# Eight sets of sums for w_out: where in the kernel they are made and written

## The chip, the cores and the metric

The kernel runs on one core of a Trainium2 chip. The core has five engines with queues of their own: TensorE (PE) for matmuls, VectorE (DVE), ScalarE (ACT), GpSimd (POOL), and SyncE (SP), which issues all of this kernel's DMAs in one order. Sixteen DMA engines carry the transfers. Each engine runs its own instructions in order, and engines wait for each other by semaphores. The metric is the device time of one execution in microseconds (us), as a median of several runs.

## The reference

Attention within chunks of 64 tokens, followed by a feed-forward layer with ELU, all in float32:

```python
# q, k, v: [8 batches, 8 heads, 576 tokens, 64], chunks of 64 tokens
scores = scale * np.matmul(q_c, k_c.transpose(0, 1, 2, 4, 3))
scores = scores - np.max(scores, axis=-1, keepdims=True)
attn = np.exp(scores)
attn = attn / (np.sum(attn, axis=-1, keepdims=True) + 1e-09)
x = np.matmul(attn, v_c)             # then reshaped to [4608 tokens, 512]
...
h = x @ w_in                          # w_in: [512, 2048]
g = np.where(h > 0.0, h, np.exp(np.minimum(h, 0.0)) - 1.0)
return g @ w_out                      # w_out: [2048, 512]
```

## The kernel before

**Numbers.** Each float32 operand of a large matmul is split into a high and a low part of a narrower float type, and a product is three matmuls (`three`, L431): high times high, high times low, low times high. The split is always the same pair of instructions: ACT copies the high part, and DVE or POOL subtracts it to get the low part.

**Blocks.** The 4608 tokens are nine blocks of 512. Three go through the plain way. The other six are three *superblocks* of two blocks each. There the two products with w_in are done by a scheme with 7 instead of 8 block products (Strassen's, in Winograd's form). For a pair g of 128-wide slices of the hidden layer (f = 2g and 2g + 1; eight pairs), `PRODUCTS` names the operands: parts and sums of w_in from `a_dram` in DRAM, and parts and sums of x. In the third superblock the product with w_out is done in the same way, and that needs *sums of w_out*.

**The sums of w_out.** `Sums` (L564) makes one set for a pair j of 128-row slices of w_out, j = 0 to 7. The steps are: `whole` twice (high plus low gives the float32 slice, 128x512), `sum` four times (differences of quarter matrices, 128x256), `high` (ACT, 128x1024), `low` (128x1024), and `write`: two DMAs of 512 KB each to `w_dram`, the high parts and the low parts. `whole` reads the low parts of w_out from `weights[0][3]`, a ring that holds eight of the sixteen slices at a time and is refilled from `lo_dram` by `load_lo` (L666) after each odd f is used. A set needs a place of 128 x 2048 floats. The other operands of the last superblock are unsummed parts, which `write_raw` ("W0" to "W5", 512 KB each) and `write_raw_low` ("L0" to "L7", 384 KB each) send to `w_dram`.

**The first two superblocks** (`for sb in range(2)`, L1363) have an order written out by hand. Each has two stages:

- *Pairs* (L1366): `FIRST_PAIR`, `SECOND_PAIR` and six times `PAIR` are strings of items. `p1` to `p7` are the seven products into two PSUM banks. Each product also issues the load of the same operand for the next pair (`load_a`, L650, 256 KB). `c` and `d` take products out of PSUM, `1` to `4` apply ELU and split the result, and `Q` is one quarter of a product with w_out. Between them runs the attention for the tokens of the next superblock, one tile of 128 tokens per pair: `l` loads q and k into one of two staging places `kept_st[0]` and `kept_st[1]` (L227, eight or sixteen small DMAs), `q` and `k` turn them, `s` multiplies them, `m E z h` make the weights and turn them with four swap DMAs (L399) at the end, `v` multiplies by v (`times_v`, L256), and `V` loads the next v (L206). In a pair the order on PE is p1, p2, p6, p5, p7, p4, p3, then s and v.
- *The second half* (`KEPT`, sixteen rows f = 0 to 15): the second block's g, kept in `g_kept`, is split (`split_kept`, L811: ACT high, then the low part on the engine that its last lines choose) and multiplied with w_out, four `Q` a row, two rows after the split. Rows also hold the attention and the preparation of the next superblock's x operands (`x...` items, L688 to L697).

Before the change, four sets (j = 0 to 3) are made in the *second* superblock's pairs: `SUMS_AT` names the items after which `do("w")` takes one more step of `combine_w_out`. Wholes and differences are on POOL, `high` on ACT, `low` on DVE, and both halves are written at once. The sets lie in rows 8 to 15 of `g_kept`. The raw parts are written in the second half of that superblock, as `RAW` says.

**The last superblock** is ordered by a planner (`Plan`, L824). Jobs have an engine or a choice of two, a cost, and the keys that they read and write; a job is due a little before the first PE job that needs it, and each engine takes the ready job that is due first. `add_sums` (L1835) adds the sets j = 4 to 7 there, staged in the place of `g_more`. The operands come through a ring of four slots of 512 KB (`load_entry`), whose first four loads are the items R0 to R3 of the second superblock's second half.

Of the kernel before, what the change touches and what calls it, by code (L numbers as in the profile page):

```python
# [20 lines left out]
def kernel(  # L21
# [542 lines left out]
    class Sums:  # L564
# [8 lines left out]
        def whole(self, i: int, engine=nc.gpsimd):  # L573
            engine.tensor_tensor(  # L574
                out=self.w[:, i], in0=w_out_slices(2 * self.j + i)[0].bitcast(F32),
                in1=self.lows[i].bitcast(F32), op=ALU.add)

        def sum(self, t: int, engine=nc.gpsimd):
            b11, b12, b21, b22 = [self.w[:, i, c * HALF:(c + 1) * HALF]
                                  for i in range(2) for c in range(2)]  # L580
            t1, t2, t3, t4 = [self.s[:, i] for i in range(4)]
            out, a, b = ((t1, b12, b11), (t2, b22, t1), (t3, b22, b12), (t4, b21, t2))[t - 1]
            engine.tensor_tensor(out=out, in0=a, in1=b, op=ALU.subtract)
# [8 lines left out]

        def write(self):
            for lo in range(2):
                nc.sync.dma_start(
                    out=w_dram[:4, self.j // 2, :, self.j % 2, lo, :].rearrange("i p w -> p i w"),
                    in_=self.place[:, lo].rearrange("p (i d) -> p i d", i=4))

    def combine_w_out():
        for j, place, lows in sums_by_hand():  # L600
            sums = Sums(j, place(), lows)
            sums.whole(0)
            yield
            sums.whole(1)
            yield
            sums.sum(1)
            sums.sum(3)
            yield
            sums.sum(2)
            sums.sum(4)  # L610
            yield
            sums.high()
            yield
            sums.low()
            sums.write()
            yield

    def sums_by_hand():
        def lows(j: int, half: int = 0):
            return [weights[half][3][:, (2 * j + i) % (NF // 2), :] for i in range(2)]  # L620

        for j, row in ((0, 8), (1, 12), (2, 8), (3, 12)):
            yield j, lambda row=row: flat(g_kept[:, row:row + 4]), lows(j)

# [16 lines left out]
    def flat(t):  # L641
        return t.rearrange("p a b -> p (a b)")
# [168 lines left out]
    def split_kept(f: int):  # L811

        if f < NF - NTT or not preparing:
            hi, lo = [flat(weights[1][3])[:, (2 * (f % NTT) + i) * TB:(2 * (f % NTT) + i + 1) * TB]
                      for i in range(2)]
        else:
            hi, lo = g_tiles()
        for _ in split_g(g_row(f), hi, lo, nc.vector if f in (0, NF - 1) or not preparing and f % 2 == 0 else nc.gpsimd):
            pass
        second(f, hi, lo)  # L820
# [174 lines left out]
    def warm(n: int):  # L995
# [3 lines left out]
        for i in range(n):  # L999
# [76 lines left out]
    )  # L1076
    RAW = {0: "L0 L1", 1: "L2 L3", 2: "W0", 4: "W1", 6: "W2", 9: "L4 L5", 10: "W3", 11: "R0 L6", 12: "W4 R1",
           13: "L7 W5", 14: "R2", 15: "R3"}
    SUMS_AT = {0: ("p3",), 1: ("p1", "p2", "p6", "p5", "d2", "p4", "p3"),
               4: ("p1", "p2", "c2", "d2"), 5: (), 6: (), 7: ()}  # L1080
    SUMS_AT[2] = SUMS_AT[3] = ("p1", "p2", "c2", "d2", "p4", "p3")

# [169 lines left out]
    attention.done |= {(n, item) for item in "qksmEVz"}  # L1252
    combining_w_out = combine_w_out()
    ring, t3_place = [], []
# [30 lines left out]
    def do(item: str):  # L1285
        if item == "C":
            next(combining, None)
        elif item == "w":
            next(combining_w_out, None)
        elif item[0] == "W":  # L1290
# [72 lines left out]
    for sb in range(2):  # L1363
        n0 = (PLAIN + 2 * sb) * TB
        run = n0, o_tiles(), a_half_place
        for g in range(NG):  # L1366
            before, pair = pair, Pair(sb * NG + g)
            for item in ((FIRST_PAIR, SECOND_PAIR)[g] if not sb and g < 2 else PAIR).split():
# [11 lines left out]
                else:  # L1380
                    do(item)
                if sb and item in SUMS_AT[g]:
                    do("w")
        halves_kept, o_last = iter(range(NF)), o_tiles()
        run = n0 + TB, o_last, b_half_place
        for f, line in enumerate(KEPT):
            for item in line.split() + (RAW.get(f, "").split() if sb else []):
                if item == "4":
                    next(pair.parts["4"], None)
                elif item == "G":  # L1390
                    split_kept(next(halves_kept))
                else:
                    do(item)

    units = {}
    NSPLIT = 7
# [414 lines left out]
    for when, (job, f, tt, hi, lo) in zip([T0 - 1 + .05 * i for i in range(4)] + [T0 - .5 + .05 * i for i in range(4)],  # L1811
# [10 lines left out]
        if last:  # L1822
# [11 lines left out]
                     [("G", 3, tt)], [])  # L1834
    def add_sums(t: float, j: int):  # L1835
        made = {}

        def begin(engine):
            made[0] = Sums(j, g_more_of(4 + j % 2), [weights[0][3][:, 2 * j + i - NF // 2, :] for i in range(2)])
            made[0].whole(0, engine)  # L1840

        place = [("G", 4 + j % 2, b) for b in range(4)]
        raw = [("s", i, l) for i in range(4) for l in range(2)] + [
            ("G", i, b) for i in (6, 7) for b in range(4)]
        half = {"DVE": (350, 423), "POOL": (700, 740)}
        plan.add(t, None, EITHER, begin, raw, place[:1])
        plan.add(t + .1, None, EITHER, lambda engine: made[0].whole(1, engine), raw, place[1:2])
        for i, (k, reads) in enumerate(((1, ()), (3, ()), (2, (("t", j, 1),)), (4, (("t", j, 2),)))):
# [6 lines left out]

    for j in range(NG // 2, NG):
        add_sums(T0 + 2 + 6 * (j - NG // 2), j)
    for s in range(2, NS):
# [31 lines left out]
```

## Time and profile before

| | before |
|---|---|
| median of 3 runs | 844.77 us (842.46 to 845.1) |
| the profiled execution: its time | 844.88 us |
| its span, first to last instruction | 842.9 us |
| mean granted TensorE clock | 0.997 |
| HBM read and written | 137.36 MB and 42.99 MB |

Where the stages lie in the span, by the chain of waits and the timeline:

| stage | us |
|---|---|
| start and the three plain blocks | 0 to 318 |
| first superblock: pairs | 318 to 447 |
| first superblock: second half | 447 to 492 |
| second superblock: pairs | 492 to 635.5 |
| second superblock: second half | 635.5 to 683 |
| last superblock | 683 to 843 |

How to read the rows of the profile further on: a timeline row is a start, a length in us, an engine, a source line, an operation, what is written from what, and a count; what stands in brackets at its end is the idle time ahead of it and who ended it. A wait row is an engine and a line, what it waited for, the us in total, how often, and the longest. SPq is SP's queue.

### The profile page before, as it was taken

To read this page: it belongs to the slowest core of one execution; us is meant where nothing else is said; L and a number is where in the kernel's file an instruction comes from. 1 tells how busy PE (TensorE), PEld (TensorE's weight loads), DVE (VectorE), ACT (ScalarE), POOL (GpSimd) and SP (SyncE) were. 2 spreads that over 40 slices of the span, in tenths; PEclk is the share of its full clock that TensorE was granted. 3 is DMA by queue.
4 is the path that set the end of the run, shared out by engine and by line. 5 is a ranking of instruction groups with operands and counts; after the bars stand their busy time and mean duration, and the time that the engine had idled before them with its cause. 6 is when DMAs were issued, how large, how long until landed. Compare 5 with 4: busy or idle time off the path is not lost.

```text
span 842.9 us, 15872 instructions
## 1 busy us (share of the span) xinstructions
PE 816.8 (97%) x5901; PEld 666.0 (79%) x5901; DVE 581.8 (69%) x832; ACT 497.9 (59%) x853; POOL 185.8 (22%) x160
## 2 busy tenths in 40 slices
PE   7899999999999999999999999898899999999997
PEld 5688888878888888888888888677788887888886
DVE  5899997666775679566666747666555269657974
ACT  5999876445554547656565446555565348676551
POOL 0000014445312120111114615541115312000100
PEclk9999999999999999999999999999999999999999
DMA  9875855856687767688878746999957779865655
GB/s 253 249 236 177 249 177 157 273 186 205 221 233 225 205 189 224 201 249 239 255 212 257 190 154 181 230 247 253 253 155 226 255 258 318 244 195 184 219 200 149
DMA packets 204972, 185.09 MB, mean 220 GB/s; under 512 B 76896, under 2 KB 186976, under 8 KB 204896
## 3 DMA queue, kind: packets, MB, share of 16 engines
q1 hardware_dynamic: 204896, 184.08, 73.9%
q8 instruction: 47, 0.77, 0.4%
q14 instruction: 29, 0.24, 0.1%
HBM read 137.36 MB, written 42.99 MB: 214 GB/s over the span
## 4 chain that ended last, share of the span: by engine, by line
PE 84%; DMA 7%; ACT 3%; SPq 3%; DVE 3%; issue 1%; DVEq 0%; ACTq 0%
PE o L434 44%; PE h L434 34%; DMA w_dram<-g_kept 2%; PE ps_a L248 2%; PE ps_a L256 2%; SPq L206 1%; DMA turned<-unturned 1%; PE h L451 1%; DMA w_dram<-g_more 1%; DMA wi_hi<-a_dram 1%; DMA st<-in_moe_w_in_dram 1%; SPq L227 1%; DVE g_more L574 1%; PE ps_a L315 1%; PE ps_a L270 0%
## 5 line engine op out<-in xcount | busy, mean ns | idle before, releaser
L434 PE MATMUL o<-wo_hi,ghi 128*128 128x512 f32 x352 | 139.0, 395 | 0.0
L434 PE MATMUL o<-wo_hi,glo 128*128 128x512 f32 x352 | 137.3, 390 | 0.0
L434 PE MATMUL o<-wo_lo,ghi 128*128 128x512 f32 x352 | 137.1, 390 | 0.0
L434 PE MATMUL h<-xhi,wi_hi 128*128 128x512 f32 x276 | 96.3, 396 | 5.0 <-DMA wi_hi<-a_dram 5.0
L434 PE MATMUL h<-xlo,wi_hi 128*128 128x512 f32 x276 | 94.6, 390 | 0.6 <-DMA wi_hi<-a_dram 0.6
L723 POOL TENSOR_TENSOR glo<-e,ghi 128x512 fp32r<-128x512 f32 x32 | 41.4, 1295 | 213.4 <-ACT ghi L721 210.8
L434 PEld LDWEIGHTS o<-wo_hi,ghi 128*128 128x128 f32 x352 | 66.0, 188 | 14.7 <-ACT ghi L476 0.4
L434 PEld LDWEIGHTS o<-wo_hi,glo 128*128 128x128 f32 x352 | 66.1, 188 | 14.4 <-DVE glo L479 0.4
L434 PEld LDWEIGHTS o<-wo_lo,ghi 128*128 128x128 f32 x352 | 66.1, 188 | 13.3
L434 PE MATMUL h<-xhi,wi_lo 128*128 128x512 f32 x180 | 70.2, 390 | 0.0
L434 PEld LDWEIGHTS h<-xhi,wi_hi 128*128 128x128 f32 x276 | 51.5, 188 | 17.4 <-ACT e L712 4.1
L434 PEld LDWEIGHTS h<-xlo,wi_hi 128*128 128x128 f32 x276 | 51.7, 188 | 11.4 <-DVE g_kept L716 1.0
L434 PE MATMUL o<-wo_hi,wo_lo 128*128 128x512 f32 x192 | 59.7, 390 | 0.0
L510 POOL TENSOR_TENSOR kept<-wi_hi,wi_lo 128x512 f32<-128x512 f32 x16 | 21.3, 1350 | 158.2 <-DMA kept<-in_k_dram 117.3
L471 DVE SCALAR_TENSOR_TENSOR e<-e,h 128x512 f32<-128x512 f32 x48 | 32.9, 685 | 27.1 <-ACT e L469 26.8
L434 PE MATMUL h<-wi_lo,wi_hi 128*128 128x512 f32 x192 | 50.6, 399 | 0.0
L762 ACT COPY kept<-h 128x512 f32<-128x512 f32 x48 | 28.2, 588 | 35.5 <-PE h L434 35.5
L434 PE MATMUL h<-wo_lo,wi_hi 128*128 128x512 f32 x192 | 48.5, 389 | 0.0
L361 DVE TENSOR_REDUCE mx<-ps_a 128x8 f32<-128x512 f32 x28 | 19.3, 689 | 39.7 <-ACT xf L420 39.0
L393 ACT COPY unturned<-turned 128x512 f32<-128x512 f32 x28 | 17.4, 621 | 49.3 <-DVE turned L388 45.2
L716 DVE SCALAR_TENSOR_TENSOR g_kept<-e,g_kept 128x512 f32<-128x512 f32 x32 | 25.9, 809 | 29.2 <-ACT e L713 29.2
L468 ACT ACTIVATE e<-h 128x512 f32<-128x512 f32 x48 | 28.7, 597 | 28.8 <-PE h L434 24.7
(201 smaller groups left out, 1814.4 us busy)
## 6 DMA issues: line engine op xcount, KB each, us to landing
wi_hi<-a_dram SPq DMA_DIRECT2D x112, 256.0 KB, 5.0
wo_lo<-lo_dram SPq DMA_DIRECT2D x36, 512.0 KB, 5.2
ring<-a_dram SPq DMA_DIRECT2D x56, 256.0 KB, 4.8
ring<-w_dram SPq DMA_DIRECT2D x28, 512.0 KB, 3.2
kept<-in_q_dram SPq DMA_DIRECT2D x100, 128.0 KB, 3.6
kept<-in_k_dram SPq DMA_DIRECT2D x100, 128.0 KB, 3.7
v_sb<-in_v_dram SPq DMA_DIRECT2D x32, 256.0 KB, 6.1
st<-in_moe_w_in_dram SPq DMA_DIRECT2D x16, 512.0 KB, 4.2
```

The lines of the kernel that those rows point to most:

```text
L206: nc.sync.dma_start(out=dst[p0:p0 + n], in_=src[b, :, s0:s0 + n, :].rearrange("h s d -> s h d"))
L248: nc.tensor.matmul(scores[halves[c], j, hp, :], lhsT=qT[halves[j], hp, halves[c]], rhs=kT[halves[j], hp, halves[c]], start=True, stop=True,)
L256: nc.tensor.matmul(x_ps[halves[j], c, hp, :], lhsT=v_sb[halves[c], 2 * hp + j, :], rhs=aT[halves[c], :, j * NK + hp], start=True, stop=True,)
L361: nc.vector.tensor_reduce(out=mx, in_=self.scores, axis=AX.X, op=ALU.max)
L393: nc.scalar.copy(out=unturned, in_=turned)
L434: nc.tensor.matmul(ps, lhsT=a, rhs=b, start=start, stop=stop, skip_group_check=onto)
L468: nc.scalar.activation(out=e, in_=h, func=AF.Relu, scale=-1.0)
L471: nc.vector.scalar_tensor_tensor(out=e, in0=e, scalar=-1.0, in1=h, op0=ALU.add, op1=ALU.max)
L510: nc.gpsimd.tensor_tensor(out=out, in0=a, in1=b, op=op)
L716: nc.vector.scalar_tensor_tensor(out=to, in0=e, scalar=-1.0, in1=c, op0=ALU.add, op1=ALU.max)
L723: engine.tensor_tensor(out=lo, in0=e, in1=hi.bitcast(F32), op=ALU.subtract)
L762: nc.scalar.copy(out=c21 if i == 4 else self.kept[i - 1], in_=x_ps)
```

## The change

The eight sets are made at other places, partly by other engines, with other staging:

- j = 2 in the first superblock's pairs 1 to 3, j = 3 in the second superblock's pairs 1 to 3. Wholes and differences are on POOL in pair 1, `high` and `low` in pair 2. The high half is written after product 3 of pair 2, the low half after product 3 of pair 3. They lie in rows 8 to 11 of `g_kept`.
- j = 4 in the first superblock's second half, on DVE, in rows 0 to 3 of `g_kept`; both halves are written at row 12.
- j = 0 and 1 begin in pair 7 of the second superblock and end in its second half (rows 2 to 8), on DVE, in the q/k staging `kept_st[0]` and `kept_st[1]`.
- j = 5, 6 and 7 in the last superblock, staged in `kept_st` in turn. (`add_sums` can also load low parts from DRAM, for j below 4; no such j is used.)
- The low parts of rows 8 to 13 of both second halves move from POOL to DVE (`VECTOR`).
- The raw writes W0 to W5 move from rows 2, 4, 6, 10, 12, 13 to rows 7, 8, 9, 11, 13, 15, and L1 to L3 one to two rows later.

```diff
-        def write(self):
-            for lo in range(2):
+        def write(self, which=(0, 1)):
+            for lo in which:
                 nc.sync.dma_start(
...
-    def combine_w_out():
...
+    early_sums = {}
+
+    def sum_step(j: int, part: str):
+        if part == "a":
+            place = kept_st[j][:, :4 * TB] if j < 2 else flat(g_kept[:, {2: 8, 3: 8, 4: 0}[j]:][:, :4])
+            early_sums[j] = Sums(j, place, [weights[0][3][:, (2 * j + i) % (NF // 2), :] for i in range(2)])
+        sums = early_sums[j]
+        if part in "ab":
+            sums.whole("ab".index(part), nc.gpsimd if j in (2, 3) else nc.vector)
+        elif part in "cd":
+            for t in ((1, 3), (2, 4))["cd".index(part)]:
+                sums.sum(t, nc.gpsimd if j in (2, 3) else nc.vector)
+        elif part == "e":
             sums.high()
-            yield
+        elif part == "f":
             sums.low()
-            sums.write()
-            yield
...
+            sums.write((0,))
+        else:
+            sums.write((1,))
...
-        for _ in split_g(g_row(f), hi, lo, nc.vector if f in (0, NF - 1) or not preparing and f % 2 == 0 else nc.gpsimd):
+        for _ in split_g(g_row(f), hi, lo, nc.vector if f in VECTOR else nc.gpsimd):
...
-    RAW = {0: "L0 L1", 1: "L2 L3", 2: "W0", 4: "W1", 6: "W2", 9: "L4 L5", 10: "W3", 11: "R0 L6", 12: "W4 R1",
-           13: "L7 W5", 14: "R2", 15: "R3"}
-    SUMS_AT = {0: ("p3",), 1: ("p1", "p2", "p6", "p5", "d2", "p4", "p3"),
-               4: ("p1", "p2", "c2", "d2"), 5: (), 6: (), 7: ()}
-    SUMS_AT[2] = SUMS_AT[3] = ("p1", "p2", "c2", "d2", "p4", "p3")
+    VECTOR = (0, 8, 9, 10, 11, 12, 13, 15)
+    MORE_PAIR = {(1, "p1"): "a", (1, "p6"): "b", (1, "p7"): "c", (1, "p3"): "d", (2, "p5"): "e", (2, "p3"): "f",
+                 (3, "p3"): "g"}
+    FIRST_SUMS = {(7, "p2"): "w0a", (7, "p6"): "w0b", (7, "p5"): "w0c", (7, "p7"): "w0d", (7, "p4"): "w1a",
+                  (7, "p3"): "w1b"}
+    MORE_KEPT = ({
+        7: "w4a", 8: "w4b", 9: "w4c", 10: "w4d", 11: "w4e", 12: "w4f w4g",
+    }, {
+        0: "L0", 1: "L1", 2: "L2 w0e", 3: "L3 w0f", 4: "w0g", 5: "w1c", 6: "w1d", 7: "w1e W0",
+        8: "w1f w1g W1", 9: "L4 L5 W2", 11: "R0 L6 W3", 12: "R1", 13: "L7 W4", 14: "R2", 15: "R3 W5",
+    })
...
-                if sb and item in SUMS_AT[g]:
-                    do("w")
+                for part in MORE_PAIR.get((g, item), "").split():
+                    do(f"w{2 + sb}{part}")
+                if sb and (g, item) in FIRST_SUMS:
+                    do(FIRST_SUMS[g, item])
...
+    LATE_SUMS = 5, 6, 7
...
-    def add_sums(t: float, j: int):
+    def add_sums(t: float, j: int, turn: int):
...
-            made[0] = Sums(j, g_more_of(4 + j % 2), [weights[0][3][:, 2 * j + i - NF // 2, :] for i in range(2)])
+        def begin():
+            made[0] = Sums(j, kept_st[turn][:, :4 * TB],
+                           [weights[0][3][:, (2 * j + i) % (NF // 2), :] for i in range(2)])
...
-        place = [("G", 4 + j % 2, b) for b in range(4)]
+        place = [("stage", turn, b) for b in range(4)]
...
-    for j in range(NG // 2, NG):
-        add_sums(T0 + 2 + 6 * (j - NG // 2), j)
+    for i, j in enumerate(LATE_SUMS):
+        add_sums(T0 + 2 + 12 * i, j, i % 2)
```

More of the change, by code (lines that the diff above doesn't have):

```diff
@@ L576, in whole, with load @@
                 in1=self.lows[i].bitcast(F32), op=ALU.add)
+        def load(self):
+            half, f = divmod(2 * self.j, NF // 2)
+            to = self.place[:, 1].rearrange("p (i d) -> p i d", i=2)
+            self.lows = [to[:, i] for i in range(2)]
+            nc.sync.dma_start(out=to, in_=lo_dram[half, :, f * DM:(f + 2) * DM].rearrange("p (f d) -> p f d", f=2))
         def sum(self, t: int, engine=nc.gpsimd):
@@ L597, in write @@
                     in_=self.place[:, lo].rearrange("p (i d) -> p i d", i=4))
-    def combine_w_out():
-        for j, place, lows in sums_by_hand():
-            sums = Sums(j, place(), lows)
-            sums.whole(0)
-            yield
-            sums.whole(1)
-            yield
[L606 to L611, printed above, removed]
+    early_sums = {}
[10 more added lines that the diff above has]
+        elif part == "e":
             sums.high()
-            yield
+        elif part == "f":
             sums.low()
-            sums.write()
[L616 to L623, printed above, removed]
+            sums.write((0,))
+        else:
+            sums.write((1,))
     def write_raw(n: int, lo: int):
@@ L1252 @@
     attention.done |= {(n, item) for item in "qksmEVz"}
-    combining_w_out = combine_w_out()
     ring, t3_place = [], []
@@ L1287, in do @@
             next(combining, None)
-        elif item == "w":
-            next(combining_w_out, None)
+        elif item[0] == "w":
+            sum_step(int(item[1]), item[2])
         elif item[0] == "W":
@@ L1386 @@
         for f, line in enumerate(KEPT):
-            for item in line.split() + (RAW.get(f, "").split() if sb else []):
+            for item in line.split() + MORE_KEPT[sb].get(f, "").split():
                 if item == "4":
@@ L1834, with load, whole @@
                      [("G", 3, tt)], [])
-    def add_sums(t: float, j: int):
+    def add_sums(t: float, j: int, turn: int):
         made = {}
-        def begin(engine):
-            made[0] = Sums(j, g_more_of(4 + j % 2), [weights[0][3][:, 2 * j + i - NF // 2, :] for i in range(2)])
+        def begin():
+            made[0] = Sums(j, kept_st[turn][:, :4 * TB],
+                           [weights[0][3][:, (2 * j + i) % (NF // 2), :] for i in range(2)])
+        def load():
+            begin()
+            made[0].load()
+        def whole(engine):
+            if not made:
+                begin()
             made[0].whole(0, engine)
-        place = [("G", 4 + j % 2, b) for b in range(4)]
+        place = [("stage", turn, b) for b in range(4)]
         raw = [("s", i, l) for i in range(4) for l in range(2)] + [
-            ("G", i, b) for i in (6, 7) for b in range(4)]
+            ("G", i, b) for i in ((4, 5) if j < NG // 2 else (6, 7)) for b in range(4)]
         half = {"DVE": (350, 423), "POOL": (700, 740)}
-        plan.add(t, None, EITHER, begin, raw, place[:1])
-        plan.add(t + .1, None, EITHER, lambda engine: made[0].whole(1, engine), raw, place[1:2])
+        if j < NG // 2:
+            plan.add(t, "SP", dma(1, 1500), load, [], place[2:])
+        plan.add(t + .1, None, EITHER, whole, raw + place[2:], place[:1])
+        plan.add(t + .15, None, EITHER, lambda engine: made[0].whole(1, engine), raw + place[2:], place[1:2])
         for i, (k, reads) in enumerate(((1, ()), (3, ()), (2, (("t", j, 1),)), (4, (("t", j, 2),)))):
```

## The prediction

> **What bounds the kernel now.** I read the page's busy times first. Then I cut the span into stages with the view of windows, and asked the view of waits what TensorE (PE) waited for in the one stage where it stands still.
>
> ```profile
> PE 816.8 (97%) x5901; PEld 666.0 (79%) x5901; DVE 581.8 (69%) x832; ACT 497.9 (59%) x853; POOL 185.8 (22%) x160
> ```
>
> PE is busy for 816.8 of the 842.9 us, and the change leaves its work as it is. So at most the 26 us in which PE idles can go, and a part of those lies at the start and the end. In the view of windows each row is a stretch: its length, then busy time and instructions of PE, PEld, DVE, ACT and POOL, the granted clock, the DMA engines' busy share, and GB/s.
>
> ```profile
> 318.00:446.00 128.00, 128.00 (x928) 104.87 (x928) 83.26 (x132) 82.44 (x141) 19.47 (x15) 1.00 0.80 230
> 446.00:508.00 62.00, 62.00 (x451) 51.13 (x443) 38.80 (x44) 29.35 (x48) 25.37 (x17) 1.00 0.69 201
> 508.00:635.00 127.00, 116.49 (x863) 93.31 (x862) 78.38 (x114) 73.90 (x123) 42.01 (x37) 1.00 0.78 215
> 635.00:690.00 55.00, 55.00 (x273) 45.55 (x266) 27.60 (x28) 21.88 (x33) 23.07 (x17) 1.00 0.79 256
> ```
>
> The pairs of the first superblock (318 to 446) and both second halves keep PE full. The pairs of the second superblock (508 to 635) lose 10.5 us. The view of waits for 500 to 640 us says to what:
>
> ```profile
> PE h L434 <- DMA wi_hi<-a_dram: 5.6, 5, 2.1
> PE ps_a L256 <- DMA turned<-unturned: 4.8, 5, 1.2
> ```
>
> Both are transfers: the operands of the products (L650) and the swap of the turned attention weights (L399). Now the same stage pair by pair, cut where the products 1 begin, after the busiest pair of the first superblock for comparison:
>
> ```profile
> 365.54:381.82 16.28, 16.28 (x132) 13.34 (x131) 10.09 (x17) 9.93 (x17) 2.60 (x2) 1.00 0.93 262
> ```
>
> ```profile
> 508.06:524.33 16.27, 16.27 (x132) 13.32 (x131) 12.40 (x17) 10.82 (x18) 10.64 (x9) 1.00 0.65 181
> 524.33:545.41 21.08, 17.28 (x133) 13.46 (x131) 14.26 (x19) 11.50 (x19) 9.85 (x9) 1.00 0.84 213
> 545.41:564.33 18.92, 17.11 (x132) 13.55 (x131) 13.12 (x17) 10.99 (x18) 9.10 (x9) 1.00 0.94 258
> 564.33:583.70 19.37, 17.00 (x132) 13.50 (x131) 11.21 (x17) 10.99 (x18) 5.26 (x7) 1.00 0.90 250
> 583.70:603.37 19.67, 17.13 (x135) 13.62 (x131) 10.10 (x16) 10.14 (x17) 3.02 (x3) 1.00 0.91 250
> 603.37:619.67 16.30, 16.30 (x131) 13.34 (x131) 9.87 (x16) 9.41 (x16) 1.56 (x2) 1.00 0.83 242
> ```
>
> An undisturbed pair takes 16.28 us. Exactly four pairs are longer, by 4.80, 2.64, 3.09 and 3.39 us: 13.9 us together. That is more than the idle 10.5, because PE's busy time in those pairs also swells, from 16.3 to about 17.1. The sync engine's (SP's) timeline shows why these four:
>
> ```profile
> 528.06 0.58 SPq L650 DMA_DIRECT2D wi_hi<-a_dram  x1
> 528.74 1.10 SPq L595 DMA_DIRECT2D w_dram<-g_kept  x2
> 529.92 1.01 SPq L650 DMA_DIRECT2D wi_hi<-a_dram  x1
> ```
>
> ```profile
> 538.26 1.61 PE L434 MATMUL h<-xhi,wi_hi 128*128 128x512 f32 x6 [2.13 <-DMA wi_hi<-a_dram]
> ```
>
> At 528.74 a set of sums, 2 x 512 KB, goes out between two loads of operands. The load at 529.92, of product 4, queues behind it. PE, whose timeline is the second fence, has stood idle for 2.13 us when it starts that product at 538.26. Three more such writes follow, one a pair. Before the first of them (508 to 524) and after the last (603 to 619) no time is lost.
>
> **The change part by part.**
>
> *Writes leave the pairs: -13.9 us, and what is left.* Of the four sets in this stage, one (j = 3) stays. Its two halves go out one pair apart, and each stands after product 3 and that product's load, so that no late operand is behind it. Sets 0 and 1 go to the second half, and 2 to the first superblock's pairs, in the same form. So the pairs hold four issues of 512 KB, one a pair, where they held eight, two a pair. What does a half cost there? The trace has no such write, so I bound it. The upper end is by size: 13.9 us for eight issues is 1.74 each, so four cost 7.0. The lower end is 0, if the queue has room. Nothing below 0 is possible, since the undisturbed pair has no PE wait left to lose. The nearest rows are those of pair 2 of the first superblock, at the place where the first half will stand:
>
> ```profile
> 368.89 0.55 SPq L206 DMA_DIRECT2D v_sb<-in_v_dram  x1
> 369.54 3.31 SPq L650 DMA_DIRECT2D wi_hi<-a_dram  x3
> 373.33 2.74 SPq L399 DMA_DIRECT2D turned<-unturned  x4
> ```
>
> Next, when times_v starts on PE, how long the swap takes to land over this superblock's pairs (the view of the tile turned), and the DMA engines in short windows:
>
> ```profile
> 381.18 0.65 PE L256 MATMUL ps_a<-turned,v_sb 64*64 64x64 f32 x32
> ```
>
> ```profile
> DMA to landing us min/median/max: 1.8/2.4/5.2
> ```
>
> ```profile
> 374.00:375.50 1.50, 1.50 (x8) 1.27 (x7) 0.90 (x2) 0.62 (x2) 0.00 (x0) 1.00 1.09 371
> 375.50:377.50 2.00, 2.00 (x11) 1.65 (x10) 2.00 (x3) 1.10 (x2) 1.30 (x1) 1.00 0.36 115
> 377.50:380.00 2.50, 2.50 (x13) 2.07 (x12) 0.95 (x2) 2.09 (x4) 0.00 (x0) 1.00 0.72 211
> ```
>
> The half will stand just ahead of 368.89. Queued behind it on SP are v's load, the next pair's loads for products 1, 2 and 6, and the swap. Issuing it takes SP about 0.55 us (half of 1.10). The three loads take 3.31 us where three plain issues take 1.7 (3 x 0.58), so SP waits 1.6 us there anyway, and the 0.55 vanish in it. The engines need 0.524 MB / 371 GB/s = 1.4 us for it. They are saturated until 375.5, then have 2.0 x 0.64 + 2.5 x 0.28 = 2.0 us free before 380. The swap's last issue ends at 376.07 (373.33 + 2.74) and lands some 2.4 us later, at 378.5, where it is wanted at 381.18: 2.7 us of slack against 1.4 us. Both margins hold, so I take the value nearest to these rows: 0.1 us a write, 0.5 us in all, and keep 0 and 7.0 for the range.
>
> At this point the Trainium skill speaks against the change: "DMA: Bandwidth & Descriptors", section "Measured (HBM→SBUF, 128 partitions, SWDGE, issued from GpSimd)", advises batching transfers to at least 1 MiB, since smaller ones pay a fixed part each. By that rule a half would cost as much as any other issue of its size, and spreading would save only by the count, eight issues to four: the 7.0 us above instead of 0.5. The trace speaks against it in so far as each of the old writes is already two issues of 512 KB; no run here shows one alone.
>
> *The sums' arithmetic.* In the first superblock's pair 1 GpSimd (POOL) gets two wholes and four differences, in pair 2 ACT a high part and DVE a low one. Pair 508.06 to 524.33 held such a load (POOL 10.64 us busy, DVE 12.40 of 16.27) and lost nothing: cost 0. The cover is the idle quarter of DVE.
>
> *Set 4 and six low parts (rows 8 to 13) on DVE in the first superblock's second half.* This is the tightest place:
>
> ```profile
> 473.54 0.62 ACT L721 CAST wo_lo<-g_kept 128x512 fp32r<-128x512 f32 x1
> ```
>
> ```profile
> 476.53 1.13 DVE L351 STREAM_TRANSPOSE qT<-kept 128x512 f32<-128x512 f32 x1
> 477.49 1.36 DVE L692 TENSOR_TENSOR xlo<-xf,xlo 128x1024 fp32r<-128x1024 f32 x1
> 478.77 1.13 DVE L351 STREAM_TRANSPOSE k_turned<-kept 128x512 f32<-128x512 f32 x1
> 481.27 2.33 DVE L692 TENSOR_TENSOR wo_lo<-xf,wo_lo 128x1024 fp32r<-128x1024 f32 x1 [1.37 <-POOL wo_lo L723]
> ...
> 487.08 1.23 DVE L692 TENSOR_TENSOR wo_lo<-xf,wo_lo 128x1024 fp32r<-128x1024 f32 x1 [1.25 <-ACT wo_lo L688]
> ```
>
> ```profile
> 481.23 3.51 POOL L723 TENSOR_TENSOR glo<-g_kept,ghi 128x512 fp32r<-128x512 f32 x2
> ```
>
> ```profile
> 685.32 1.89 DVE L574 TENSOR_TENSOR g_more<-wo_hi,wo_lo 128x512 f32<-128x512 f32 x3
> ```
>
> ```profile
> 481.42 0.62 PE L434 MATMUL o<-wo_hi,wo_lo 128*128 128x512 f32 x2
> ```
>
> These are timelines of ACT, DVE, POOL, DVE again and PE. Neighbours on DVE overlap by some 0.08 us, so three 512-wide operations in 1.89 us are 0.61 each, a turn is 0.96 (477.49 - 476.53), and a 1024-wide one 1.15 alone (1.23 less the overlap), but 2.33 beside POOL. From 474.16, when ACT has the high part of row 8, DVE now does: low 8, a whole of set 4, xT3's low, the turn of q, low 9, the other whole, xB22's low, the turn of k, low 10. That is 5 x 0.61 + 2 x 1.15 + 2 x 0.96 = 7.3 us, so low 10 is there at about 481.4, and PE takes it at 481.42: no room, and no loss. After that POOL no longer doubles the 2.33 us, and DVE catches up. I take 0.3 us. Below 0 is impossible (PE waits for nothing there now); the upper end is one low part beside one busy POOL instruction, 1.3 us, or 1.6 in all. Set 4's 1 MB goes out at row 12, where the stage's DMA share is 0.69; behind it on SP stand lo loads that are issued over 16 us ahead of their use.
>
> *Sets 0 and 1 in the second superblock's second half: +2 MB.* DVE is busy 27.60 of 55 us there. A set is two 512-wide operations, four half as wide (0.34 each, my estimate from 0.61) and one 1024-wide: 3.7 us. Two sets and six low parts, 11 us, lie beside PE. For the transfers:
>
> ```profile
> 657.00:663.00 6.00, 6.00 (x29) 4.95 (x28) 2.17 (x2) 2.42 (x4) 2.59 (x2) 1.00 0.37 120
> 663.00:676.00 13.00, 13.00 (x59) 10.78 (x58) 4.54 (x4) 3.54 (x5) 3.82 (x3) 1.00 0.96 301
> ```
>
> 1 MB at 301 GB/s is 3.5 us. Set 1 meets the free 0.63 x 6 = 3.8 us of the first row; set 0 is out before, in a stage with a share of 0.79. I take 0; the other end is 3 us, if the last raw write (moved to row 15) puts the ring's loads behind. Staging in the q/k buffers waits for nothing: their last tile is turned in pair 6.
>
> *Last superblock: three sets instead of four, spread.* The view of waits from 700 us on has one line:
>
> ```profile
> PE o L434 <- DVE g_kept L1457: 0.4, 1, 0.4
> ```
>
> This wait comes right after the burst of sums on DVE: -0.4, or 0 if it has another cause.
>
> The profiled execution took 844.88 us, 2.0 of it outside the span, and 0.1 over the median of 844.77. **Sum:** 844.9 - 13.9 + 0.5 + 0.3 + 0 - 0.4 = 831.4 us, and 831.3 against the median.
>
> **The rivals.**
>
> *Each issue keeps its price.* The halves cost 1.74 us each: 831.3 - 0.5 + 7.0 = 837.8. For it: the busiest undisturbed pair already has a share of 0.93. Against: the drained queue after 375.5, and the better place.
>
> *The second half and the ring come late.* The moved raw write and sets 0 and 1 delay the last superblock's first loads by up to 3 us, and DVE's tight rows add 1.6: about 835. Against: the free queue above.
>
> *The writes are not the cause.* If POOL's sums, which slow DVE (14.26 against 10.09 us busy), made the swap late, the same sums would do so in both superblocks, and the time stays near 844. Against: the pair from 508 has the busiest POOL and no loss, and the one from 583.70 has DVE at 10.10 and loses 3.4.
>
> *Slower: SP is held by a write whose low part is late.* The half stands in SP's queue until DVE has made the low part, which it gets between product 3 and the next sum. If that is over 1.6 + 2.7 = 4.3 us after SP's arrival, everything behind it (v, three operands, the swap) reaches PE late, in four pairs over two superblocks. At the dearest price seen, 4.80 each: 831.3 - 0.5 + 19.2 = 850.0. Against: DVE idles a third of such a pair, and the high part is made half a pair earlier.
>
> **How the numbers follow.** Forecast 831.3: 0.70. Price by issue: 0.13. Late second half or ring: 0.08. Writes not the cause: 0.05. SP held: 0.04. About 0.3% (2.5 us) is what a measurement of this kernel can tell from no change, so faster is 0.70 + 0.13 + 0.08 = 0.91, same 0.05, slower 0.04. The range goes down by the spread of the runs before (the lowest is 2.3 us under the median) to 829.0 and up to the price by issue, 838.0; it leaves out the last two cases.
>
> **What would show it.** Right: pairs of 16.28 us in both superblocks, with no PE wait on wi_hi or turned; two issues of L595's form a superblock in the pairs, one pair apart. Wrong: pairs 3 and 4 longer than 16.3 us (price by issue), PE waits on DVE's low parts near row 10 of the first second half, PE waits on ring loads at the last superblock's start, or SP waiting on DVE ahead of a write.

## The result and the profile after

The median fell from 844.29 us (4 runs, 842.46 to 845.1) to 837.29 us (4 runs, 835.11 to 837.75): a ratio of 0.9915, with a 95% interval of 0.9891 to 0.9939. That is 7.0 us; 13.5 were forecast. The profiled execution took 835.11 us, its span 833.3.

First the page's busy times of the kernel after, in the columns shown of before:

```profile
PE 815.4 (98%) x5901; PEld 666.6 (80%) x5901; DVE 587.8 (71%) x859; ACT 497.7 (60%) x853; POOL 152.7 (18%) x133
```

POOL's 33 us less are the sums and low parts that went to DVE. DVE's busy time rose by 6.0 us only. Next the view of waits of after, from 490 to 640 us, and then from 660 us on:

```profile
PE ps_a L256 <- DMA turned<-unturned: 2.2, 3, 1.2
PE h L434 <- ACT kept L762: 0.7, 1, 0.7
```

```profile
PE h L434 <- DMA ring<-a_dram: 0.9, 1, 0.9
PE o L434 <- DMA ring<-w_dram: 0.4, 1, 0.4
```

The wait for operands (5.6 us before) is gone, and of the wait for the swap (4.8 us) 2.2 us are left. Three small waits are new. Below are the windows of after, now cut where times_v (L256) begins, since a late swap shows there. I call them stretches; stretch n ends with times_v of pair n. The first line runs from inside the first superblock's second half (with set 4 and rows 8 to 13) to the end of the second superblock's pair 0; the others are stretches 1 to 7 of the second superblock:

```profile
462.23:505.87 43.64, 43.64 (x263) 35.78 (x258) 30.99 (x39) 20.62 (x32) 5.97 (x4) 1.00 0.70 198
505.87:522.15 16.28, 16.28 (x144) 13.33 (x138) 10.30 (x17) 9.94 (x17) 8.29 (x8) 1.00 0.66 189
522.15:538.52 16.37, 16.37 (x144) 13.38 (x135) 11.14 (x18) 10.82 (x18) 2.59 (x2) 1.00 0.70 193
538.52:556.37 17.85, 16.84 (x138) 13.66 (x131) 11.01 (x18) 9.95 (x18) 2.60 (x2) 1.00 0.89 243
556.37:574.34 17.97, 16.80 (x131) 13.61 (x131) 10.10 (x16) 10.38 (x18) 2.59 (x2) 1.00 0.89 242
574.34:591.04 16.70, 16.63 (x130) 13.56 (x134) 9.22 (x15) 9.64 (x17) 2.58 (x2) 1.00 0.90 253
591.04:607.32 16.28, 16.28 (x143) 13.34 (x138) 10.10 (x17) 9.93 (x17) 2.59 (x2) 1.00 0.84 248
607.32:624.12 16.80, 16.10 (x112) 12.75 (x103) 12.12 (x22) 9.63 (x17) 2.84 (x2) 1.00 0.22 72
```

Four places hold what is missing. Stretches 2 to 5 are 0.09, 1.57, 1.69 and 0.42 us over 16.28: 3.77 us. Stretch 7 takes 16.80 us, and took 15.77 before: 1.03. The ring's loads cost 0.92 and 0.43 us. That is 6.15 us.

The stretches before, cut in the same way, were 20.77, 18.80, 19.41, 19.09 and 17.25 us long: 13.92 over. Up to the scores (L248) of the first superblock's pair 1, with which the change begins, PE's work is the same in both kernels, yet it got there at 348.10 us before and at 346.39 after. So single executions are compared below by the **rest**: the span less that start. It was 842.9 - 348.1 = 494.8 us before and 486.9 after.

All runs in one table, from the same windows. Loss in the first and the second superblock's pairs is what their stretches take over 16.28 us each; "ring" is all waits of PE after 660 us, most of them for the ring's loads. Each row is one profiled execution, e1 to e9 have no other, and two executions of after lie 3.2 us apart in rest; so below the rows of a trace count more than its time.

| kernel | time | rest | first superblock, loss | second: stretches 2 to 6, loss | stretch 7 | ring |
|---|---|---|---|---|---|---|
| before | 844.88 | 494.8 | 0 | 13.92 | 15.77 | 0.4 |
| after | 835.11 | 486.9 | 0 | 3.77 | 16.80 | 1.3 |
| after, second trace (e11) | 841.38 | 490.1 | 1.44 | 6.2 | 16.80 | 1.0 |
| e1 | 831.46 | 482.9 | 0 | 1.57 | 15.76 | 0.6 |
| e2 | 843.65 | 495.0 | 0 | 14.08 | 15.77 | 0.3 |
| e3 | 833.57 | 485.2 | 0 | 1.68 | 16.75 | 1.7 |
| e4 | 836.43 | 485.6 | 1.89 | 1.38 | 16.75 | 0.9 |
| e5 | 843.11 | 493.1 | 0 | 12.45 | 15.76 | 0.3 |
| e6 | 834.34 | 483.8 | 1.14 | 0 | 16.75 | 1.2 |
| e7 | 834.62 | 485.2 | 1.73 | 0.91 | 16.75 | 1.1 |
| e8 | 834.72 | 484.0 | 2.01 | 1.40 | 15.77 | 0 |
| e9 | 836.78 | 485.7 | 0 | 2.01 | 16.80 | 1.7 |
| e10 | 832.88 | 482.4 | 0.20 | 0.94 | 15.76 | 0.4 |

### The profile page after: what moved, and what is told of

It reads as the page before. It is cut to its first block, busy times and chain, and to the rows that moved or that the text cites. A ratio compares the mean times of both kernels' runs of the same rounds, so it can differ in the third digit from the quotient of the medians.

```text
span 833.3 us, 15864 instructions
## 1 busy us (share of the span) xinstructions
PE 815.4 (98%) x5901; PEld 666.6 (80%) x5901; DVE 587.8 (71%) x859; ACT 497.7 (60%) x853; POOL 152.7 (18%) x133
## 4 chain that ended last, share of the span: by engine, by line
PE 90%; DMA 4%; ACT 2%; SPq 2%; DVE 1%; issue 1%; DVEq 0%; ACTq 0%
PE o L434 46%; PE h L434 38%; PE ps_a L248 2%; PE ps_a L256 2%; SPq L206 1%; DMA turned<-unturned 1%; DMA ring<-a_dram 1%; PE h L451 1%; DMA v_sb<-in_v_dram 1%; DMA st<-in_moe_w_in_dram 1%; DMA ring<-w_dram 1%; PE ps_a L315 1%; PE ps_a L270 0%; ACT e L712 0%; ACT xhi L425 0%
## 5 line engine op out<-in xcount | busy, mean ns | idle before, releaser
L762 ACT COPY kept<-h 128x512 f32<-128x512 f32 x48 | 28.1, 586 | 32.9 <-PE h L434 32.7
L716 DVE SCALAR_TENSOR_TENSOR g_kept<-e,g_kept 128x512 f32<-128x512 f32 x32 | 22.6, 705 | 32.6 <-ACT e L713 32.6
```

The lines of the kernel that those rows point to most:

```text
L716: nc.vector.scalar_tensor_tensor(out=to, in0=e, scalar=-1.0, in1=c, op0=ALU.add, op1=ALU.max)
L762: nc.scalar.copy(out=c21 if i == 4 else self.kept[i - 1], in_=x_ps)
```

## The experiments

### Writes or arithmetic (e1, e2)

Two theories of the long pairs of before: the queue of writes, or the sums on POOL and DVE. e1 keeps the arithmetic there and moves the writes away; e2 keeps the writes and takes the arithmetic away.

```diff
-            sums.write()
...
+            if not sb and f in (6, 9, 12, 14):
+                for lo in range(2):
+                    nc.sync.dma_start(
+                        out=w_dram[:4, (6, 9, 12, 14).index(f) // 2, :, ...
```

> The kernel before, with all arithmetic of the four sets in place, but without their writes in the second superblock's pairs; 1 MB of high parts of w_out goes to the same places in w_dram at rows 6, 9, 12 and 14 of the first superblock's second half, instead of the sums. Theory W (the writes cost the 13.9 us): pairs 2 to 5 of the second superblock fall from 21.1, 18.9, 19.4 and 19.7 us to 16.28, except that pair 2 may keep the 0.65 us that the changed kernel loses there before any write; the span falls by 13 us or more. Theory A (POOL's sums, which hold DVE up, make the swap late): the four pairs stay over 18 us and the span within 3 us of before.

```diff
-            sums.whole(0)
...
-            sums.high()
...
-            sums.low()
```

> The kernel before, with the four sets' writes at their places in the second superblock's pairs, but without their wholes, differences, high and low parts; what is written is whatever lies in those rows of g_kept. Theory W: the four pairs stay long, some 13 us over 4 x 16.28 together, with PE waiting on the operands and the swap. Theory A: they fall to 16.28. If both have a share, the excess is between, and this run and the one without writes together say how it divides.

Windows of e1 (stretches 2 to 4), then of e2 (2 and 3):

```profile
522.39:538.86 16.47, 16.47 (x144) 13.26 (x135) 12.89 (x18) 10.54 (x19) 9.18 (x8) 1.00 0.68 193
538.86:555.82 16.96, 16.90 (x143) 13.48 (x138) 13.38 (x18) 10.79 (x19) 9.34 (x9) 1.00 0.85 247
555.82:572.80 16.98, 16.84 (x145) 13.19 (x139) 12.69 (x19) 10.80 (x19) 6.06 (x7) 1.00 0.88 248
```

```profile
522.51:543.43 20.92, 18.07 (x145) 14.35 (x135) 10.42 (x18) 10.04 (x17) 2.59 (x2) 0.92 0.79 205
543.43:562.64 19.21, 17.01 (x131) 13.53 (x131) 10.67 (x17) 10.36 (x18) 2.59 (x2) 1.00 0.95 251
```

In e1 POOL still works 9 us a stretch and DVE nearly 13, and 1.57 us are lost. In e2 POOL has 2.59 us, and 14.08 are lost. The writes are the cause; the arithmetic costs nothing that shows. e1's gain in rest is 494.8 - 482.9 = 11.9 us.

### The place of a write in the pair (e5)

The prediction held that after product 3 a write delays no late operand. e5 puts before's 1 MB writes there, three of them.

```diff
-        for j, row in ((0, 8), (1, 12), (2, 8), (3, 12)):
+        for j, row in ((0, 12), (1, 8), (2, 12)):
...
+    SUMS_AT[1] = SUMS_AT[2] = SUMS_AT[3] = ("p1", "p2", "c2", "d2", "p4", "p3")
```

> The kernel before, with three of its four sets (0, 1, 2) made a little later, so that the 1 MB write stands after product 3 at the end of pairs 1, 2 and 3 instead of ahead of product 4's load; set 3's place in w_dram gets high parts of w_out at row 14 of the first superblock's second half. In the kernel before, the first three writes cost 4.8, 2.6 and 3.1 us. If the place is what cost: each now costs 1.4 to 1.9 us, as the whole writes after product 3 of the changed kernel's variant did, some 5 us together, and no PE wait on the operands of L650 is left, only waits on the swap. If only the bytes count: 10 us together.

The only wait of PE from 490 to 625 us, and stretches 2 to 4:

```profile
PE ps_a L256 <- DMA turned<-unturned: 6.9, 3, 4.1
```

```profile
523.76:544.32 20.56, 16.49 (x143) 13.32 (x135) 12.98 (x20) 11.92 (x21) 9.98 (x10) 0.96 0.71 204
544.32:563.81 19.49, 19.15 (x131) 15.45 (x131) 10.95 (x17) 10.35 (x17) 6.20 (x7) 0.86 0.87 252
563.81:583.14 19.33, 16.84 (x130) 13.64 (x131) 10.54 (x17) 10.60 (x18) 3.55 (x3) 1.00 0.86 249
```

No wait for operands is left; the swap, which stands behind them in SP's queue, is late instead, and 12.45 us are lost for three writes. In the stretch from 544.32 PE is busy for 19.15 of 19.49 us at a granted clock of 0.86: its work ran slower after the stall. Summed over stretches 2, 3 and 5 (0.04 x 20.56 + 0.14 x 19.49 + 0.09 x 18.19) that is 5.2 us by estimate, which leaves some 7.3, or 2.4 a write. **The place moves the wait from the operands to the swap; it doesn't remove it.** Neither theory had the three writes cost this much.

### Is it the half write, or is the swap late anyway (e3, e6, e9)?

SP's timeline of after shows how the two superblocks differ. The first fence ends with the swap for times_v at 363.19, the second with the swaps for times_v at 538.52 and at 554.80 (had it been on time, 538.52 + 16.28):

```profile
336.24 2.98 SPq L399 DMA_DIRECT2D turned<-unturned  x4
...
341.27 4.37 SPq L227 DMA_DIRECT2D kept<-in_q_dram  x8
345.72 3.67 SPq L227 DMA_DIRECT2D kept<-in_k_dram  x8
...
356.13 3.57 SPq L399 DMA_DIRECT2D turned<-unturned  x4
```

```profile
514.30 2.48 SPq L399 DMA_DIRECT2D turned<-unturned  x4
...
517.50 3.88 SPq L227 DMA_DIRECT2D kept<-in_q_dram  x8
521.42 4.80 SPq L227 DMA_DIRECT2D kept<-in_k_dram  x8
...
532.78 3.57 SPq L399 DMA_DIRECT2D turned<-unturned  x4
...
544.69 0.54 SPq L601 DMA_DIRECT2D w_dram<-g_kept  x1
...
545.88 5.30 SPq L650 DMA_DIRECT2D wi_hi<-a_dram  x3
551.27 3.17 SPq L399 DMA_DIRECT2D turned<-unturned  x4
```

In both, a tile that lies across two batches is loaded with sixteen DMAs, some 8 to 9 us of SP's time. In the first superblock (`SECOND_PAIR`) the swap ahead of them goes out 10.7 us before times_v (363.19 - 16.28 = 346.91), in the second (`PAIR`) only 7.85 us before it (522.15). So the sixteen loads end 2.5 and 4.1 us after times_v, and SP is 1.6 us later in the second. I call this the lag. The next swap is fully issued at 359.70 and at 536.35. With the median landing time of 2.4 us that the prediction quotes, it lands 1.1 us before it is wanted in the first, and 0.2 us too late in the second. Then the half write comes, the three loads behind it take 5.30 us, and the swap is issued by 554.44. With the same 2.4 us it lands 2.0 us too late; stretch 3 is 1.57 us long over.

e3 leaves the lag and takes the half writes away:

```diff
-            for lo in which:
+            for lo in which if self.j != 3 else ():
...
+            if not sb and f in (4,):
+                for lo in range(2):
+                    nc.sync.dma_start(
+                        out=w_dram[:4, 3 // 2, :, 3 % 2, lo, :]...
```

> The changed kernel, without the two half writes of set 3 in the second superblock's pairs 2 and 3; 1 MB of high parts of w_out goes there at row 4 of the first superblock's second half instead of the sums. In the changed kernel pairs 2, 3 and 4 there take 16.93, 17.62 and 18.13 us between their scores. If the half writes still cost time: pairs 3 and 4 fall to 16.28, pair 2, whose wait comes before the first half write, keeps its 0.65 us, and the span falls by about 3 us. If they are free and the second superblock is late for another reason: all three stay within 0.3 us.

e6 leaves the half writes and takes the lag away:

```diff
-        for p0, b, s0, n in pieces_of(n0, U):
+        for p0, b, s0, n in pieces_of(n0 - (C if n0 == 31 * P else 0), U):
```

> The changed kernel, with q and k of tile 31 loaded as eight DMAs of 128 KB in place of sixteen of 64 KB (the tokens are those 64 ahead, so its result is another; the bytes are the same). Theory L: the second superblock loses where the first does not because its pair 1 issues the swap 3 us later in the pair and then the sixteen loads, so that SP enters pair 2 late; with eight loads SP is some 4 us earlier, pair 2 takes 16.28 us in every case and pairs 3 and 4, with their half writes, fall to under 16.6 each. If L is wrong, pairs 3 and 4 still lose 1.3 us or more each.

Windows of e3 (stretches 2 to 4), then of e6 (the longest stretch of the first superblock's pairs, then 2 to 4 of the second's):

```profile
522.35:539.97 17.62, 16.48 (x145) 13.37 (x135) 12.04 (x19) 11.07 (x19) 2.59 (x2) 1.00 0.67 179
539.97:556.59 16.62, 16.61 (x131) 13.56 (x135) 9.22 (x15) 9.78 (x17) 2.59 (x2) 1.00 0.90 253
556.59:572.87 16.28, 16.28 (x144) 13.33 (x139) 10.10 (x17) 9.93 (x17) 2.59 (x2) 1.00 0.85 237
```

```profile
381.85:398.85 17.00, 16.82 (x144) 13.63 (x135) 10.46 (x18) 9.92 (x17) 2.60 (x2) 1.00 0.96 256
...
525.68:541.96 16.28, 16.28 (x143) 13.34 (x138) 11.05 (x18) 10.80 (x18) 2.59 (x2) 1.00 0.84 232
541.96:558.24 16.28, 16.28 (x143) 13.34 (x138) 10.19 (x17) 9.92 (x17) 2.59 (x2) 1.00 0.94 262
558.24:574.52 16.28, 16.28 (x143) 13.34 (x138) 10.10 (x17) 9.93 (x17) 2.59 (x2) 1.00 0.90 248
```

e3 loses 1.68 us with no write in the stage. e6 loses nothing with both half writes in it, once the tile is loaded with eight DMAs. The lag without a write stands in e1, e7 and e8 too, and costs 0.9 to 1.7 us in the four. So **the lag alone has a price, and the half writes cost 2.1 us more in after because they meet a swap whose slack the lag has used up.** That they are free without the lag is so in e6 alone. In e6 the first superblock's halves cost 1.14 us, though, and 0 in after: there too the margin is small, and an execution falls on one side of it or the other.

e9 takes the lag away without touching the tokens: the sixteen loads are split, eight after product 1.

```diff
+                items = items.replace("m p1 c1", "m p1 l1 c1").replace("Q l p7", "Q l2 p7")
```

> The changed kernel, with the sixteen loads of tile 31 in the second superblock's pair 1 taken apart: the eight of q go out after product 1, at the start of the pair, where SP waits, and the eight of k stay at their place. Bytes, issues and result are as in the changed kernel. Theory L (SP enters pair 2 late because all sixteen come after the swap): pairs 2 to 4 of the second superblock lose 3.8 us in the changed kernel and 0 to 0.6 here, with both half writes in place. If L is wrong and the run with single pieces was fast because eight issues fewer are fewer: they still lose 2 us or more.

Stretch 4 of e9:

```profile
557.68:575.59 17.91, 16.46 (x144) 13.41 (x135) 10.98 (x18) 10.54 (x18) 2.59 (x2) 1.00 0.85 228
```

Stretches 2 and 3, with the first half write in the latter, fall to 16.28, as the theory has it; behind the second half write PE waits 1.45 us for the swap. The gain was 1.8 us in place of the 3.2 or more expected, and the 2.01 us that are left stand at the mark that was set for "L is wrong". SP's timeline of e9 in that stretch:

```profile
563.51 0.55 SPq L601 DMA_DIRECT2D w_dram<-g_kept  x1
...
564.71 5.66 SPq L650 DMA_DIRECT2D wi_hi<-a_dram  x3
570.46 3.14 SPq L399 DMA_DIRECT2D turned<-unturned  x4
```

The swap is fully issued at 573.60, and times_v was due at 573.96 (557.68 + 16.28): a margin of 0.36 us. Where PE waited for a swap at the start of a stretch's times_v, in any of these runs, times_v began 1.8 to 2.4 us after the swap's last issue, so some 2 us are needed. The same margin for the swaps of stretches 2, 3 and 4, from the timelines of SP and PE (where there are half writes, one stands early in stretch 3 and one early in stretch 4):

| kernel, superblock | half writes | margin, 2 | 3 | 4 |
|---|---|---|---|---|
| before, first | none | 3.34 | 5.11 | 5.38 |
| after, first | two | 3.49 | 3.57 | 2.47 |
| e11, first | two | 3.91 | 1.99 | 0.91 |
| e3, second, with the lag | none | 0.71 | 2.95 | 3.54 |
| after, second, with the lag | two | 2.08 | 0.36 | 0.25 |
| e6, second, no lag | two | 5.37 | 4.77 | 3.90 |
| e9, second, no lag | two | 3.80 | 2.84 | 0.36 |
| e10, second, no lag | two | 3.59 | 2.53 | 1.71 |

Without writes the margin grows from pair to pair; with a half in each of two pairs it ends lower than it began, and the second half meets what the first has left. So the lag is not the whole cause: in e9 the margin starts well, and the two halves use it up. Why the second takes 2.5 us of it in e9 and 0.8 in e10, with the same issues, stays open.

### Halves, or both at once (e4)

```diff
-            sums.write((0,))
+            sums.write((0, 1) if j in (2, 3) else (0,))
...
-            sums.write((1,))
+            sums.write(() if j in (2, 3) else (1,))
```

> The changed kernel, with both halves of sets 2 and 3 written at once after product 3 of pair 2, in both superblocks, and nothing after product 3 of pair 3. If the bytes count: the first superblock's pair 3, which has 2 us of free queue, takes 1.4 us more transfer without a loss or loses under 1 us; the second superblock's pair 3 becomes 1.5 to 2 us longer than 17.62 and pair 4 shorter than 18.13, the sum about as before. If halving and placing the writes are what made the first superblock free, its pair 3 loses over 1 us here.

PE's timeline of e4, one wait for the swap in each superblock:

```profile
383.65 1.05 PE L256 MATMUL ps_a<-turned,v_sb 64*64 64x64 f32 x32 [1.31 <-DMA turned<-unturned]
...
560.26 1.05 PE L256 MATMUL ps_a<-turned,v_sb 64*64 64x64 f32 x32 [0.76 <-DMA turned<-unturned]
```

1.89 and 1.38 us are lost, 3.27 together, against 3.77 in one trace of after and 7.6 in the other. The first superblock's 1.89 us is what was expected if halving had made that superblock free (0 in after); but e11, with halves, loses 1.44 there. In the second superblock the loss was expected to stay, and it fell. So writing a set in two halves a pair apart isn't shown to be worth anything; that four sets became one in this stage is.

### Both sets in the first superblock; the sums on POOL; the late sums held (e7, e8)

e7 moves set 3 to the first superblock's pairs. e8 does two things more: the wholes and differences of sets 0 and 1 go to POOL, and the last superblock's sums wait until its pairs 0, 2 and 4 have passed product 4.

```diff
+                   (2, "p1"): "w3a", (2, "p6"): "w3b", (2, "p7"): "w3c", (3, "p1"): "w3d", (3, "p5"): "w3e",
+                   (4, "p3"): "w3f", (5, "p3"): "w3g"}, {})
```

> The changed kernel, with set 3 also made in the first superblock (POOL in pairs 2 and 3, rows 12 to 15 of g_kept, its half writes after product 3 of pairs 4 and 5), so that the second superblock's pairs hold no write. If halves are free in the first superblock: its pairs 2 to 7 all take 16.28 us, the second superblock's pairs 3 and 4 fall from 17.6 and 18.1 to 16.28, pair 2 loses 0 to 1.7 us as in the runs so far, and the stretch from the first superblock's pair 1 to the end falls from 486.9 to about 484 us. If a half costs 1.74 us wherever it stands, the first superblock loses that in two more pairs.

```diff
-            sums.whole("ab".index(part), nc.gpsimd if j in (2, 3) else nc.vector)
+            sums.whole("ab".index(part), nc.vector if j == 4 else nc.gpsimd)
...
+            ("G", i, b) for i in ((4, 5) if j < NG // 2 else (6, 7)) for b in range(4)] + [("G", after, 1)]
...
-        add_sums(T0 + 2 + 12 * i, j, i % 2)
+        add_sums(T0 + 16 + 14 * i, j, i % 2, 2 * i)
```

> As the last one, with two more edits: the wholes and differences of sets 0 and 1 on POOL instead of DVE, and the three late sets held back until the last superblock's pairs 0, 2 and 4 have passed product 4. Expected: the second superblock's pair 7 falls from 16.8 to 15.8 us (the PE wait of 0.7 us on ACT goes, if DVE's sums caused it), and the PE wait of 0.9 us on the ring near the last superblock's start goes, if the three sets' writes, which in the changed kernel all go out in its first 20 us, caused it; if the backlog of the second half caused it, it stays. The stretch from the first superblock's pair 1 to the end: about 482 us.

e7 loses 1.73 us for four halves in the first superblock and 0.91 in the second, where no write is left. Together 2.64 us, against 3.77 in after; the 0.91 is the lag again (the swap's margin in stretch 2 is 1.88 us). Neither of the two prices set, 0 and 1.74 us a half, came out: it is 0.4. In e8 stretch 7 is back at 15.77, and PE waits for nothing from 660 us on: both edits do what they say, 1.0 us each. Its pairs lost 3.4 us, so the rest is 484.0 and not the 482 expected.

### After once more, and the three repairs together (e11, e10)

> The changed kernel once more, for a second trace of it. Its wait on ACT in the second superblock's pair 7 (0.7 us) and on the ring near 691 us (0.9 us) should be there again, since both stood in every trace of a kernel that has those parts as they are; the loss of its pairs 2 to 4 in the second superblock (3.8 us in the first trace) and that of the first superblock's pairs 3 and 4 (0 there, 1.1 in the run with single pieces) hang on margins of a microsecond, so I expect 2 to 4 us for the two together.

> The three repairs together on the changed kernel: tile 31's loads taken apart, the wholes and differences of sets 0 and 1 on POOL, the late sets held back until the last superblock's pairs 0, 2 and 4 have passed product 4. From the first superblock's pair 1 to the end the changed kernel takes 486.9 us; less 3.3 us (pairs 2 to 4), 1.0 us (pair 7) and 0.9 us (ring) gives 481.7, or 482.8 if the first superblock's halves cost 1.1 us as in the run with single pieces. The time is then about 832 us against 844 before, a ratio of 0.985 to 0.987, some 5 us under the changed kernel.

e11 is the kernel after, unchanged. The waits on ACT (0.70 us) and on the ring (1.00) are there again; the pairs of both superblocks lose 7.6 us in place of the 2 to 4 expected. Its stretch 5, and that stretch's beginning in three short windows:

```profile
579.70:598.00 18.30, 18.24 (x131) 14.71 (x134) 9.35 (x15) 9.53 (x16) 2.57 (x2) 0.91 0.86 244
```

```profile
580.00:582.00 2.00, 1.95 (x34) 1.64 (x35) 0.59 (x1) 0.59 (x1) 1.01 (x1) 0.74 0.97 258
582.00:584.00 2.00, 2.00 (x6) 1.55 (x5) 0.80 (x2) 0.59 (x2) 0.00 (x0) 0.50 0.86 237
584.00:586.00 2.00, 2.00 (x9) 1.64 (x8) 0.78 (x2) 1.65 (x3) 0.00 (x0) 0.91 0.78 188
```

PE had waited 1.45 us for the swap; the clock then fell to half. That makes 0.09 x 18.30 = 1.65 us of the 6.2 lost. The rest, 490.1 against 486.9 us, shows how far two executions of one kernel lie apart when its swap has no slack.

e10 is e9 with e8's last two edits. It took 832.88 us at the median (5 runs, 831.01 to 834.41) against 843.61 of before (9 runs, 842.21 to 844.75): a ratio of 0.9872, with an interval of 0.9853 to 0.9891. Its rest is 482.4 us, within the 481.7 to 482.8 expected. Its five times lie below all of before's, and below the four of after, which were taken at another time. Stretches 4, 5 and 7:

```profile
557.05:573.77 16.72, 16.46 (x143) 13.41 (x135) 10.54 (x18) 9.93 (x17) 2.60 (x2) 1.00 0.90 254
573.77:590.55 16.78, 16.64 (x131) 13.58 (x134) 9.67 (x16) 10.03 (x17) 2.59 (x2) 1.00 0.85 249
...
606.83:622.59 15.76, 15.76 (x111) 12.82 (x102) 8.07 (x14) 9.80 (x17) 9.87 (x9) 1.00 0.21 69
```

## Why the prediction was half right

The direction and the cause were right, and the range held the time. The sum was 6.0 us short: 831.3 against 837.3. By the rest, the forecast is 494.8 - 13.9 + 0.5 + 0.3 - 0.4 = 481.3, and after took 486.9: 5.6 us. Step by step:

- **The writes leave the pairs, -13.9 us: right.** e1 and e2 show that they are the cause; e1 leaves 1.57 us of it in place.
- **"0.1 us a write, 0.5 us in all": the step that failed**, with 3.77 us in its place (7.6 in e11). It was worked out from "the nearest rows", which were the first superblock's, and carried to the second unlooked-at. (They are the right rows for the first superblock's first half, though the pair on PE there is pair 3 and not 2; and the window from 446 to 508 holds the second superblock's pair 0 besides a second half. Neither moves the sum.) There the swap ahead of the first half has -0.2 us to spare, not 2.7. The rows that say so, the sixteen loads after a later swap, stood in the trace of before too. e3 sizes the lag alone at 1.7 us, and e6, without it, gives 0 for both halves. In the first superblock the term came out in four of six traces (0 in after, e3 and e9, 0.2 in e10; 1.14 and 1.44 in e6 and e11), but its working didn't: the wait in the three loads doesn't swallow the write, since behind the first half they took SP 4.75 us in after and 6.96 in e11, not 3.31; and each half was weighed against the full slack, where the second meets what the first has left of it (e9).
- **"after product 3 ... so that no late operand is behind it": true, and of no use.** In e5 the operands are on time and the swap isn't.
- **Price by issue** gave 837.8 us, close to the time measured, and pairs over 16.3 us were its mark, which came. But an issue has no price of its own: the same half costs 0 in e6's second superblock, and about 1 us with the lag. The time agrees by luck, because other terms were missed. As to the rule of the Trainium skill ("DMA: Bandwidth & Descriptors", section "Measured (HBM→SBUF, 128 partitions, SWDGE, issued from GpSimd)"; its table is of loads issued from GpSimd, the halves are writes issued from SP), the 7.0 us that the prediction drew from it lies between the 3.77 and the 7.6 of after's two traces; e4, with both halves at one place, lost no more than either.
- **The first superblock's second half, 0.3 us: right.** The stretch that holds set 4 and the six low parts took 43.64 us, and 43.48 before. PE waits for nothing in it.
- **Sets 0 and 1 "lie beside PE", 0: 1.03 us too low.** The sums on DVE (12.12 of 16.80 us busy in stretch 7) hold up ACT, and with it the copy of a product out of PSUM (L762), for which product 4 of pair 7 waits 0.70 us. On POOL they cost nothing (e8, e10).
- **The ring, "I take 0", and -0.4 for the late sums: some 1.3 us too low.** The free queue that was counted on was gone. Windows of after, and SP's timeline around the superblock's start:

```profile
646.30:652.30 6.00, 6.00 (x28) 4.96 (x27) 4.70 (x5) 2.56 (x5) 0.00 (x0) 1.00 0.80 274
652.30:665.30 13.00, 13.00 (x59) 10.77 (x58) 6.42 (x7) 3.58 (x5) 0.00 (x0) 1.00 1.05 326
...
687.00:692.00 5.00, 4.08 (x18) 3.10 (x17) 4.29 (x7) 4.53 (x8) 0.00 (x0) 1.00 1.09 343
```

```profile
676.06 1.02 SPq L601 DMA_DIRECT2D w_dram<-kept  x2
...
681.22 1.10 SPq L601 DMA_DIRECT2D w_dram<-kept  x2
682.41 5.74 SPq L1279 DMA_DIRECT2D ring<-a_dram  x6
688.69 2.35 SPq L601 DMA_DIRECT2D w_dram<-kept  x2
```

  Before's wait of 0.4 us is gone, as forecast. The second half starts 10.67 us earlier in after (the times_v just ahead of it begins at 624.12, and at 634.79 before), so the first two rows are the 657 to 663 and 663 to 676 of the prediction: shares of 0.80 and 1.05, and 0.37 and 0.96 before. The third holds the wait for the ring, one of the prediction's own signs of being wrong: the three late sets, which nothing held back, all went out between 676 and 691 us, the last between the ring's own loads. Between 676 and 700 us the ring's loads land in 6.6 us at the median in after and in 3.4 in e8. Held back, the sets leave no wait there (e8, e10). The profile of e7 and e9 puts the wait at this place down to DVE, and holding a set back moves its arithmetic along with its writes, so the two aren't told apart by a run. The 0.43 us come at 821 us, far behind, and stand in e10 too (0.41).

The three mis-sized terms are 3.27, 1.03 and 1.35 us, and the second half was 0.14 less: 5.5 of the 5.6 us. What stays open is why the same half takes more of the swap's margin in one execution than in another. The stretches of 16.9 us in e7, which have no wait in the view, have margins of 1.4 us: times_v begins 0.2 us late and lasts 0.95 to 1.09 us in place of 0.65, probably waiting for the swap's four transfers one by one, which counts as busy.

## What to carry to other kernels

A write costs what the slack of the last thing behind it in its queue doesn't cover. Work that slack out for each place from that place's own rows, issue by issue, and not from a similar pair of another loop; and where writes follow each other, take off what the earlier ones have used. Where it is near zero, more issues ahead (here eight more loads) are as dear as the write itself, and the time begins to scatter from run to run.

## What the runs showed of the hardware

After a stall of PE the granted clock can fall to 0.50. By windows of 1 us it did so for about 3.4 us after stalls of 2.72 (e2), 2.44 (e5) and 1.45 us (e11), and for about 6.8 us, twice that, from late in a stall of 4.07 us on (e5). It didn't after one of 2.13 us (before), nor after another of 1.45 us (e9). The page "TensorE: Matmul & The Clock Gate" of the Trainium skill (section "Part 1: The HAM clock gate (the "warmup" mystery)") has half the clock and a window of about 3.4 us that runs free, and the 0.50 and the 3.4 us agree; that a stall well under one window can be enough is shown here by the 1.45 us of e11. And the first 350 us, the same work for PE in all these kernels, ended between 346.4 and 349.5 us.
